# Linear attention with a gated network beside it: keys and values of two token tiles in seven block products, in rounds of two tiles

## The chip, the cores and the metric

The kernel runs on one core of one Trainium2 chip. The metric is device time in microseconds (us), the median over several runs; a second number, the span, is the time from the first to the last recorded instruction in one profiled execution.

## The reference

2048 tokens with 512 features go through a layer norm. From the normed tokens come two branches, and the output joins them. Cut to what is computed:

```python
xn = _layernorm(x)                                   # (1, 2048, 512)
qkv = xn @ wqkv                                      # H = 32 heads of Dh = 16
pq, pk = q @ w_phi, k @ w_phi                        # per head, 16 x 16
phi = concat([softmax(p), softmax(-p)], axis=-1)     # for pq and for pk
kv  = einsum("bhsf,bhsd->bhfd", phi_k, v)            # sums over all tokens
z   = einsum("bhsf->bhf", phi_k)
o   = (phi_q @ kv) / (phi_q @ z + 1e-6)
s   = o.reshape(B, S, D) @ wo
gate, up = xn @ W_gate, xn @ W_up                    # F = 1376
g   = silu((relu(gate) * up) @ W_down)
out = x + s * g
```

Everything is fp32 (the names here are shortened).

## The kernel before

**Numbers in two parts.** A TensorE (PE) matmul takes operands of type fp32r, with fewer bits than fp32. Each operand is split into a high part (a copy that rounds, on ScalarE, called ACT) and a low part (the difference, on VectorE, called DVE, or on GpSimd, called POOL). `mm3` issues three matmuls for each 128-deep piece of the contraction: low x high, high x low, high x high.

**Order.** A wrapper, `InOrder`, keeps all instructions of an engine in the order in which the program calls them. A planner, `Clock` (line 63), estimates at build time when each engine is free, with fixed costs and rates; background generators (weight preparation, queries) are advanced at `pace.pump()` where their engine is due. So the order is settled when the kernel is built, and an instruction that waits holds up whatever stands behind it on its engine. All instructions are recorded under one line (L59), so views are read by the names of tiles.

**Phase 1** runs over 16 tiles of 128 tokens (n = 0 to 15; two blocks of 512 tokens are taken alternately, `PAIRS`). Ahead of the loop (line 1091) a prologue folds `w_phi` into the key and query weights (`fold`, WK and WQ) and turns the first tiles. For each tile:

- `norm_stats`, `norm_scale`, `norm_apply`: mean and variance by two ACT passes, a power of -1/2 on POOL, and a scaled copy `xn`. Tiles 0 to 3 use `norm_vector`, with bn statistics on DVE.
- `turn` (line 320): transposes on PE into PSUM (`pxT`), high part by ACT, a full copy `xf` by ACT, low part by DVE (`lo_xt`). `sums_x` (327) makes, for each pair of tiles, four sums of the transposed blocks on POOL (`sa`, `sb`), and `sums_hi` and `sums_lo` split them. XT holds eight planes: four blocks of x (A21, A22, A11, A12) and four combinations S1 to S4. They are what the seven-product scheme of phase 2 needs.
- `project(n, WK, "pk")` and `project(n, WV, "pv")` (359): 12 matmuls of 128x512 each.
- `exponents` (391): largest and smallest of each group of 16 on DVE (`mx`), two differences (`ek`). Then ACT's exp, and in `features` (407) the value's split (`vhl`), the sum of each group (`sm`), its reciprocal written into the PSUM bank of pv, and the weighting `ek<-ek,pv`.
- `features_split` (430): high part of the features by ACT, low part by POOL (`phl`, 128x1024), and a DMA on POOL's queue that adds the features into `zacc`.
- `kv_products` (438): 16 matmuls into four PSUM banks (`pkv`), which are held from tile 0 to the end of phase 1, so that four banks rotate for everything else. The products of tile n come three tiles later from n = 10 on (`LATER = 9`), two tiles later before that.
- `query(n - 1)` (364): 12 matmuls, 24 for the first two tiles, stored by DMA.

**Phase 2** is two halves of 1024 tokens. Each runs over 11 blocks of the hidden features (f = 0 to 10): `gate_up` does gate and up together in seven block products of 6 matmuls (`pa`, `pb`, `pc`, `pd`), then `down` (`py`); the queries' features and products (`q_pair`) run beside it, and output tiles (`pso`) follow.

**Weights of phase 2.** `f_load` (457) loads the raw block f, `f_prep` (480) makes combinations (`tab`, `wa` to `wd`) and splits them, low parts on POOL, and spills the result to DRAM for half 1. `all_preps` (1073) orders that: blocks f = 2 and 3 (`AHEAD`) are prepared first, in phase 1, spilled, and loaded again when half 0 comes to them; f = 0 and 1 from tiles 12 and 15 on (`START`); the others one block ahead in half 0.

Of the kernel before, what the change touches and what calls it, by code (L numbers as in the profile page):

```python
# [7 lines left out]
F32 = mybir.dt.float32  # L8
# [5 lines left out]
P = 128  # L14
# [30 lines left out]

class InOrder:
# [113 lines left out]
def layer_kernel(ctx: ExitStack, tc: tile.TileContext, x, wkT, wqT, wv, wo, wf, cst, out):  # L160
# [24 lines left out]
    def f32(t):  # L185
        return t.bitcast(F32)
# [64 lines left out]
        return lambda: split(*map(by_parity, w[k]), even_first(p))  # L251


    mhalf = sb.tile([P, 96], F32, name="mhalf")[:, 0:1]
    XT = sb.tile([P, 8, 2, 2, BT], F32R, tag="XT", name="XT")
    pace.shared = XT.name
    XN, XF, SF = {}, {}, {}

    def norm_stats(n):
        xt = X.pop(n)  # L260
        xn = u2((P, D), "xn")
        sm, ss, rs, bias = small(1, "lm"), small(1, "lv"), small(1, "lr"), small(1, "lb")
        nc.scalar.activation(xn, xt, AF.Copy, scale=-1.0 / D, accum_out=sm)
        nc.scalar.activation(xn, xt, AF.Square, bias=sm, accum_out=ss)
        XN[n] = xn, xt, bias, rs, sm, ss

    def norm_scale(n):
        xn, xt, bias, rs, sm, ss = XN[n]
        nc.vector.tensor_scalar(rs, ss, 1.0 / D, 1e-5, op0=ALU.mult, op1=ALU.add)
        nc.gpsimd.tensor_tensor(rs, rs, mhalf, op=ALU.pow)  # L270

    def norm_apply(n):
        xn, xt, bias, rs, sm, ss = XN[n]
        nc.vector.tensor_scalar(bias, sm, rs, None, op0=ALU.mult)
        nc.scalar.activation(xn, xt, AF.Identity, bias=bias, scale=rs)
        XN[n] = xn

    def norm_vector(n):

        xt = X.pop(n)  # L280
        st, mv, rs = small(6, "bs", 2), small(2, "bm", 2), small(1, "br", 2)
        nc.vector.bn_stats(st, xt)
        nc.vector.bn_aggr(mv, st)
        nc.vector.tensor_scalar(rs, mv[:, 1:2], 1e-5, None, op0=ALU.add)
        nc.gpsimd.tensor_tensor(rs, rs, mhalf, op=ALU.pow)
        XN[n] = u2((P, D), "xn"), xt, mv, rs

    def norm_vector_apply(n):
        xn, xt, mv, rs = XN[n]
        for c in [slice(0, 256), slice(256, D)] if n == 0 else [slice(0, D)]:  # L290
            nc.vector.tensor_scalar(xn[:, c], xt[:, c], mv[:, 0:1], rs, op0=ALU.subtract, op1=ALU.mult)
        XN[n] = xn

    def cols(n):
        i = order[n][1]
# [21 lines left out]
    def lo_xt(n, p):  # L317
        add(nc.vector, xt_part(n, 1), p, f32(xt_part(n, 0)), ALU.subtract)

    def turn(m, full=True):  # L320
        p = transpose_x(m)
        hi_xt(m, p)
        if full:
            full_xt(m, p)
        return m, p

    def sums_x(n):

        x0, x1 = XF.pop(n - 1), XF.pop(n)
        sa, sb_ = u2((P, 2, 2, P), "sa"), u2((P, 2, 2, P), "sb")  # L330
        add(nc.gpsimd, sa[:, 0], x1[:, 0], x1[:, 1])
        add(nc.gpsimd, sb_[:, 0], x0[:, 0], x1[:, 0], ALU.subtract)
        add(nc.gpsimd, sa[:, 1], sa[:, 0], x0[:, 0], ALU.subtract)
        add(nc.gpsimd, sb_[:, 1], x0[:, 1], sa[:, 1], ALU.subtract)
        SF[n] = sa, sb_

    def sums_hi(n):
        for s, c in zip(SF[n], (S1, S3)):
            nc.scalar.activation(XT[:, c:c + 2, 0, :, cols(n)], s, AF.Copy)

    def sums_lo(n):
        for s, c in zip(SF.pop(n), (S1, S3)):
# [64 lines left out]
    def features(n, e, raised, pv, between):  # L407
# [14 lines left out]
        if n:  # L422
            features_scale(n, e, pv)

    def features_scale(n, e, pv):
# [29 lines left out]
    DONE = set()  # L455

    def f_load(f):
        if f == AHEAD[-1]:
# [21 lines left out]
    def f_prep(f, keep=True):  # L480
# [17 lines left out]
        yield "scalar", ta  # L498
        nc.scalar.activation(wb[0], ta, AF.Copy)
        put(f, 2, wb[0])  # L500
        yield "gpsimd", wa[0]
        for c in range(2):
            add(nc.gpsimd, wa[1][:, c], rg[c][:, :, 0, :], f32(wa[0][:, c]), ALU.subtract)
# [11 lines left out]
        yield "gpsimd", wc[0]  # L515
        add(nc.gpsimd, wc[1], tb, f32(wc[0]), ALU.subtract)
        put(f, 5, wc[1])
        fd = u2((P, D), "fdh", F32R), u2((P, D), "fdl", F32R)
        yield "scalar", rd
# [5 lines left out]
        yield "gpsimd", fd[0]  # L525
        add(nc.gpsimd, fd[1], rd, f32(fd[0]), ALU.subtract)
        put(f, 8, fd[1])
        if keep:
            FT[f], WD[f] = [wa, wb, wc, wd], fd
# [505 lines left out]
    for n in range(3, 7):  # L1035
        load_x(n)
    norm_vector_apply(0)
    px = turn(0, False)
    folds = [fold(WK, wk_raw[:, k, :], k) for k in range(2)]
    lo_xt(*px)  # L1040
    folds[0]()
# [16 lines left out]
        wv_lo(k)  # L1058
    norm_vector(2)
    full_xt(*px)  # L1060
    px = turn(1)
    lo_xt(*px)
# [5 lines left out]
    sums_x(1)  # L1068
    folds[0]()
    folds[1]()  # L1070
    norm_vector_apply(3)

    def all_preps():
        for f in AHEAD:
            f_load(f)
            yield 30,
            yield from f_prep(f, False)
        f_load(0)
# [12 lines left out]
    for n in range(N):  # L1091
        at[0] = n
        if n + 7 < N:
            load_x(n + 7)
        if n == 2:
            preps = pace.add(all_preps(), 0, 3)
        if 1 < n < N - 4:
            norm_apply(n + 4)
        if 0 < n < N - 5:
            norm_scale(n + 5)  # L1100
        if n > 1:
            pk = project(n, WK, "pk")
        if n > LATER:
            kv_products(n - 3)
            pace.pump()
        turned = [turn(n + LEAD)] if 1 < n < N - LEAD else [turn(3)] if n == 1 else []
        pace.pump()
        if turned and turned[0][0] % 2:
            sums_x(turned[0][0])
        pv = project(n, WV, "pv")  # L1110
        pace.pump()
        if n == 0:
            features(0, early, True, pv, lambda: None)
            pk = project(1, WK, "pk")
            norm_stats(4)
            norm_scale(4)
            lo_xt(*turn(2))
            features_scale(0, early, pv)
            norm_stats(5)
            sums_hi(1)  # L1120
            norm_apply(4)
            norm_scale(5)
            early = exponents(pk)
        else:
            if n == 1:
                norm_apply(5)
            features(n, early if n == 1 else exponents(pk), False, pv, lambda: [lo_xt(*t) for t in turned])
            if n == 1:
                features_split(0)
                sums_lo(1)  # L1130
            query(n - 1)
            pace.pump()
            if n == 1:
                lo_xt(*turn(4))
            if n % 2 == 0 and n - 1 < N // 2:
                pace.later(4, lambda n=n: spill_x(n - 1))
        if n + 6 < N:
            norm_stats(n + 6)
        if n % 2 and n + 2 < N:
            sums_hi(n + 2)  # L1140
        if n:
            features_split(n)
        if n % 2 and n + 2 < N:
            sums_lo(n + 2)
        if 2 <= n < LATER:
            kv_products(n - 2)
            pace.pump()


    kvacc, zB, kvhl = [None] * 3  # L1150
# [5 lines left out]
    kvt = u4((P, NG, P), "kvt")  # L1156
    nc.vector.memset(kvt, 0.0)
    q_load(0)
    for n in (N - 3, N - 2):
        kv_products(n)  # L1160
    query(N - 1)
    pace.pump()

    def state():
# [216 lines left out]
```

## Time and profile before

| | us |
|---|---|
| median of 3 runs | 563.39 |
| lowest, highest | 563.32, 564.13 |
| profiled execution | 562.88 |
| its span | 561.1 |
| tiles 2 to 15 of phase 1 (39.35 to 161.93) | 122.58 |
| half 0, from the first gate-up matmul (166.59) to half 1's first (354.95) | 188.36 |

The profile is one execution, on the one core. Busy time of an engine counts its instructions, not its waits. In rows of groups, `out<-in` names tiles, then come sizes (partitions x elements) and count; after the bar stand total busy time in us and the mean of one in ns, after the next bar the idle time ahead of them and what ended it. In rows of the timeline and the chain the first number is the start in us, the second the duration; a duration of a matmul is its latency, and one that follows another of 128x512 starts about 0.227 us later. In window rows each engine's busy time is followed by its number of instructions, then come the granted clock, the busy share of the DMA engines and GB/s. A row of DMA issues ends with the size in KB and the median time from issue to landing.

### The profile page before, as it was taken

How to read it: one execution, taken by the hardware profiler on the slowest of the kernel's cores; microseconds unless marked ns; L12 is line 12 of the kernel's file. 1: busy time of each engine (PE TensorE's matmuls, PEld its weight loads, DVE VectorE, ACT ScalarE, POOL GpSimd, SP SyncE). 2: the span in 40 equal slices, each digit the busy share in tenths (PEclk: the TensorE clock that was granted, in tenths of full speed). 3: DMA queues.
4: the chain of work that ended last, by engine and by line, in shares of the span. 5: the costliest groups of instructions: out<-in, count | busy, mean ns of one | idle time of the engine just before them, and what ended most of it. 6: DMA issues, size and time to landing. Idle time of an engine off the chain costs nothing.

```text
span 561.1 us, 8197 instructions
## 1 busy us (share of the span) xinstructions
PE 555.5 (99%) x2618; PEld 465.0 (83%) x2618; DVE 386.2 (69%) x584; ACT 303.1 (54%) x543; POOL 404.6 (72%) x347
## 2 busy tenths in 40 slices
PE   8999999999999999999999999999999999999997
PEld 8888888888888888888888888887888888888886
DVE  5978777676657897799963432799883948665323
ACT  3898687765555557456464151235465555644510
POOL 1689987899888487997978333473568786888473
PEclk9999999999999999999999999999999999999999
DMA  8358999855599817979779999991755765559874
GB/s 285 132 157 238 269 270 324 245 153 166 150 304 321 313 61 261 356 266 285 269 250 322 331 388 410 370 396 47 202 187 193 244 206 183 157 179 320 252 210 165
DMA packets 84539, 137.98 MB, mean 246 GB/s; under 512 B 7824, under 2 KB 34320, under 8 KB 83600
## 3 DMA queue, kind: packets, MB, share of 16 engines
q1 hardware_dynamic: 81040, 125.33, 64.7%
q0 software_dynamic: 3312, 12.06, 11.1%
q8 instruction: 21, 0.34, 0.2%
q14 instruction: 22, 0.18, 0.1%
q10 hardware_dynamic: 144, 0.07, 0.0%
HBM read 76.87 MB, written 52.69 MB: 231 GB/s over the span
## 4 chain that ended last, share of the span: by engine, by line
PE 93%; DVE 3%; DMA 2%; issue 0%; SPq 0%; POOL 0%
PE py L59 21%; PE pd L59 10%; PE pa L59 9%; PE pb L59 8%; PE pv L59 8%; PE pk L59 8%; PE pq L59 8%; PE pso L59 8%; PE pc L59 6%; PE pkv L59 3%; PE pnum L59 3%; PE pxT L59 1%; PE pfold L59 1%; DMA pql<-pq 1%; DMA wd<-ws 1%; DVE eq L59 1%
## 5 line engine op out<-in xcount | busy, mean ns | idle before, releaser
L59 PE MATMUL py<-fdh,hl 128*128 128x512 f32 x176 | 68.5, 389 | 0.0
L59 PE MATMUL py<-fdh,hh 128*128 128x512 f32 x176 | 68.5, 389 | 0.0
L59 PE MATMUL py<-fdl,hh 128*128 128x512 f32 x176 | 68.5, 389 | 0.0
L59 PE MATMUL pa<-XT,wa 128*128 128x512 f32 x264 | 67.0, 389 | 0.0
L59 PEld LDWEIGHTS pa<-XT,wa 128*128 128x128 f32 x264 | 49.6, 188 | 10.3
L59 DVE TENSOR_TENSOR y<-py,y 128x512 f32<-128x512 f32 x40 | 27.5, 689 | 36.5 <-PE py L59 36.5
L59 POOL TENSOR_TENSOR phl<-ek,phl 128x1024 fp32r<-128x1024 f32 x15 | 36.1, 2409 | 10.7 <-ACT phl L59 10.7
L59 PE MATMUL pv<-wvh,XT 128*128 128x512 f32 x128 | 43.5, 401 | 0.0
L59 PE MATMUL pk<-wkh,XT 128*128 128x512 f32 x128 | 42.4, 392 | 0.0
L59 POOL TENSOR_TENSOR ez<-eq,zB 128x1024 f32<-128x1024 f32 x16 | 38.5, 2415 | 4.4 <-ACT eq L59 2.0
L59 POOL TENSOR_TENSOR hl<-t,hh 128x512 fp32r<-128x512 f32 x16 | 20.8, 1298 | 27.3 <-ACT hh L59 26.3
L59 PE MATMUL pq<-XT,wqh 128*128 128x512 f32 (+1 forms) x144 | 40.3, 366 | 0.0
L59 PEld LDWEIGHTS py<-fdh,hh 128*128 128x128 f32 x176 | 33.0, 188 | 6.9
L59 PEld LDWEIGHTS py<-fdl,hh 128*128 128x128 f32 x176 | 33.0, 188 | 6.8
L59 PEld LDWEIGHTS py<-fdh,hl 128*128 128x128 f32 x176 | 33.0, 188 | 6.8
L59 POOL TENSOR_TENSOR y<-y,ys 128x512 f32<-128x512 f32 x24 | 30.9, 1291 | 9.6 <-ACT ys L59 9.6
L59 PE MATMUL pd<-XT,wd 128*128 128x512 f32 x132 | 33.8, 390 | 0.5 <-DVE t L59 0.5
L59 PE MATMUL pd<-XT,wc 128*128 128x512 f32 x132 | 33.8, 389 | 0.0
L59 POOL TENSOR_TENSOR ol<-of,oh 128x512 fp32r<-128x512 f32 (+1 forms) x13 | 20.2, 1596 | 18.9 <-ACT oh L59 18.9
L59 PE MATMUL pc<-XT,wb 128*128 128x512 f32 x132 | 33.7, 389 | 0.0
L59 PE MATMUL pb<-XT,wb 128*128 128x512 f32 x132 | 33.5, 389 | 0.0
L59 POOL TENSOR_TENSOR pTl<-ez,pTh 128x1024 fp32r<-128x1024 f32 x10 | 24.0, 2400 | 8.4 <-ACT pTh L59 8.4
(174 smaller groups left out, 1559.2 us busy)
## 6 DMA issues: line engine op xcount, KB each, us to landing
zacc<-ek POOLq DMA_DIRECT2D x15, 512.0 KB, 5.8
xts<-XT SPq DMA_DIRECT2D x4, 1792.0 KB
XT<-xts SPq DMA_DIRECT2D x7, 1024.0 KB, 20.4
wa<-ws SPq DMA_DIRECT2D x26, 256.0 KB, 3.2
wb<-ws SPq DMA_DIRECT2D x26, 256.0 KB, 4.8
wc<-ws SPq DMA_DIRECT2D x26, 256.0 KB, 5.1
ws<-wa SPq DMA_DIRECT2D x22, 256.0 KB, 4.0
ws<-wb SPq DMA_DIRECT2D x22, 256.0 KB, 4.2
```

What stands on the lines that cost most here:

```text
L59: return self.tc.keep_in_program_order(op(*a, **k))
```

## The change

Tiles 0 and 1 stay as they were but for details. From tile 2 on the loop goes by pairs, `pair(m)` for m = 1 to 7, with n = 2m and n + 1.

- In the first two pairs (m = 1, 2) keys and values of both tiles are four projections of 12 matmuls, as before. From m = `FIRST` = 3 (tile 6, the seventh) they are seven blocks of 6 matmuls: two of x's blocks with keys' weights give `py`, four combinations S1 to S4 meet weights T0 to T2 and half of WV, and A22 meets T3. ACT copies partial results to where two sums grow from one start (`px<-py`, `va`, `vb`), and DVE adds `pz` to `va` and to `vb`.
- T0 to T3, combinations of key and value weights and their parts, are made by steps listed in `PLAN` (ten on DVE, ten on POOL, eight on ACT; 128x512 each) in pairs 1 to 3.
- The order in a pair: first half of keys, two blocks (or values of n + 1), second half of keys, exponents, third block, kv(n - 2), turn of n + 3, query(n - 1), kv(n - 1), A22, exponents, S4, turn of n + 4, query(n). Features of the second tile are done at the start of the next pair.
- The norm is done in place (`xt`; ACT's first passes write into one `junk` tile), the second tile of a pair takes bn statistics on DVE from m = 3 on, and one power serves both tiles.
- `sums_x` is two DVE differences that read PSUM and two POOL sums; the full copy by ACT is made for even tiles only.
- The reciprocal of the groups' sums stays in SBUF (`rc`), exp is one instruction of 1024, and in the seven-product rounds the value's low part is made by POOL.
- `AHEAD` is empty: f = 2 and 3 are prepared in half 0 like the others. f = 0 and 1 start at tiles 14 and 15. `sums_of` gives low sums of weights to DVE or POOL: from tile 14 on whichever the planner sees free first (with 5000 units against DVE in `lighter`), in turns before that.

```diff
-AHEAD = (2, 3)
-LATER = 9
-START = (12, 15)
+AHEAD = ()
+FIRST = 3
+PLAN = {(1, "sums"): "vc50 vc51", (1, "split a"): "gc00", ...}
+START = (14, 15)
-A21, A22, A11, A12, S1, S2, S3, S4 = range(8)
+A21, A22, A11, A12, S3, S2, S1, S4 = range(8)
...
+    def turned(n, p):
+        lo_xt(n, p)
+        if n % 2:
+            sums_x(n, p)
+    def sums_x(n, p):
+        a, b = XF.pop(n - 1), u2((P, 2, 2, P), "sb")
+        add(nc.vector, b[:, 0], a[:, 0], p[:, 0], ALU.subtract)
+        add(nc.vector, b[:, 1], p[:, 1], b[:, 0], ALU.subtract)
+        SF[n] = b, a
+    def sums_more(n):
+        b, a = SF[n]
+        add(nc.gpsimd, a[:, 0], a[:, 0], b[:, 1])
+        add(nc.gpsimd, a[:, 1], a[:, 1], b[:, 1], ALU.subtract)
...
+    def features_k(n, e):
+        sm, rc = small(64, "sm", 2), small(64, "rc", 2)
+        nc.vector.tensor_reduce(sm, groups(e), op=ALU.add, axis=AX.X)
+        nc.vector.reciprocal(rc, sm)
+        nc.vector.tensor_tensor(groups(e), groups(e), rc.unsqueeze(2).to_broadcast([P, 64, DH]), op=ALU.mult)
+        EK[n] = e
...
-        yield "gpsimd", wb[0]
-        add(nc.gpsimd, wb[1], ta, f32(wb[0]), ALU.subtract)
+        yield from sums_of(wb[1], ta, f32(wb[0]), ALU.subtract, wb[0])
...
+    def sums_of(o, a, b, op=ALU.subtract, *need):
+        engine = lighter()
+        if at[0] < N - 2:
+            turns[0] += 1
+            engine = ("gpsimd", "vector")[turns[0] % 2]
+        yield engine, *(need or (a, b))
+        add(getattr(nc, engine), o, a, b, op)
+    def lighter(n=512):
+        return min(("vector", "gpsimd"), key=lambda e: max(pace.free[e], pace.now) + pace.FIXED[e] + pace.RATE[e] * n + (e == "vector") * 5000)
...
+    def pair(m):
+        n, c = 2 * m, cols(2 * m)
+        at[0] = n
+        def block(p, s, w, first):
+            mm3(p, lambda k: (XT[:, s, 0, k, c], XT[:, s, 1, k, c]), rows(w), range(2), first)
+            pace.pump()
+        if m <= NP // 2:
+            pace.later(4, lambda: spill_x(n - 1))
+        seven = m >= FIRST
+        py = ps(name="pk")
+        if seven:
+            block(py, A11, WK[:2], True)
+            px = ps(name="pk")
+            nc.scalar.activation(px, py, AF.Copy)
+        else:
+            mm3(py, xt_cols(n), rows(WK), range(KD))
+        if m > 1:
+            features_k(n - 1, EB.pop())
+        t_steps(m, "start")
+        pz = ps(name="pv")
+        if seven:
+            block(pz, S1, T[0], True)
+            block(px, S2, T[1], False)
+            va = u2((P, D), "va")
+            nc.scalar.activation(va, px, AF.Copy)
+        else:
+            mm3(pz, xt_cols(n + 1), rows(WV), range(KD))
...
+        if news:
+            norm_stats(*news, bn=m > 2)
+        if seven:
+            block(py, A12, WK[2:], False)
+        ea = exponents(py)
+        if seven:
+            block(px, S3, T[2], False)
+            vb = u2((P, D), "vb")
+            nc.scalar.activation(vb, px, AF.Copy)
+            add(nc.vector, vb, pz, vb)
+        else:
+            vb = pz
...
+        kv_products(n - 2)
+        pace.pump()
+        at[0] = n + 1
+        if n + 3 < N:
+            t = turn(n + 3)
+        exp_all(ea)
+        features_v_hi(n + 1, vb)
...
+        query(n - 1)
+        features_k(n, ea)
...
+        features_split(n)
+        t_steps(m, "split a")
+        kv_products(n - 1)
+        pace.pump()
+        if seven:
+            block(px, A22, T[3], False)
+        else:
+            px = project(n + 1, WK, "pk")
+        eb = exponents(px)
+        if seven:
+            block(pz, S4, WV[2:], False)
+            add(nc.vector, va, pz, va)
+        else:
+            va = project(n, WV, "pv")
+        if n + 4 < N:
+            t = turn(n + 4)
+            if n + 8 < N:
+                load_x(n + 8)
+        exp_all(eb)
+        t_steps(m, "turned")
+        if n + 4 < N:
+            turned(*t)
+        features_v_hi(n, va)
+        features_v_lo(n, va, nc.gpsimd if seven else nc.vector)
+        EB.append(eb)
+        query(n)
+        t_steps(m, "end")
+        pace.pump()
```

More of the change, by code (lines that the diff above doesn't have):

```diff
@@ L251, in fold @@
         return lambda: split(*map(by_parity, w[k]), even_first(p))
[L254 removed]
+    mhalf = sb.tile([P, 96], F32, name="mhalf")[:, 0:2]
     XT = sb.tile([P, 8, 2, 2, BT], F32R, tag="XT", name="XT")
@@ L500, in f_prep @@
         put(f, 2, wb[0])
-        yield "gpsimd", wa[0]
         for c in range(2):
-            add(nc.gpsimd, wa[1][:, c], rg[c][:, :, 0, :], f32(wa[0][:, c]), ALU.subtract)
+            yield from sums_of(wa[1][:, c], rg[c][:, :, 0, :], f32(wa[0][:, c]), ALU.subtract, wa[0])
         put(f, 1, wa[1])
@@ L514, in f_prep @@
         nc.scalar.activation(wd[:, 0], b22, AF.Copy)
-        yield "gpsimd", wc[0]
-        add(nc.gpsimd, wc[1], tb, f32(wc[0]), ALU.subtract)
+        yield from sums_of(wc[1], tb, f32(wc[0]), ALU.subtract, wc[0])
         put(f, 5, wc[1])
@@ L524, in f_prep @@
         put(f, 6, wd)
-        yield "gpsimd", fd[0]
-        add(nc.gpsimd, fd[1], rd, f32(fd[0]), ALU.subtract)
+        yield from sums_of(fd[1], rd, f32(fd[0]), ALU.subtract, fd[0])
         put(f, 8, fd[1])
@@ L1073, in all_preps, with t_steps @@
+    def t_steps(m, where):
+        for what in PLAN.get((m, where), "").split():
+            STEPS[0](what)
     def all_preps():
@@ L1077, in all_preps @@
             yield from f_prep(f, False)
+        while at[0] < START[0] - 1:
+            yield 3,
         f_load(0)
@@ L1090, in layer_kernel @@
     at = [0]
-    for n in range(N):
+    for n in range(2):
         at[0] = n
-        if n + 7 < N:
-            load_x(n + 7)
-        if n == 2:
+        load_x(n + 7)
+        if n == 1:
             preps = pace.add(all_preps(), 0, 3)
-        if 1 < n < N - 4:
-            norm_apply(n + 4)
-        if 0 < n < N - 5:
+            t_prep()
+        if n > 0:
             norm_scale(n + 5)
[L1101 to L1109, printed above, removed]
+        tn = turn(3) if n else None
         pv = project(n, WV, "pv")
@@ L1124, in layer_kernel @@
         else:
[L1125 to L1130, printed above, removed]
+            norm_apply(5)
+            features(n, early, False, pv, lambda: turned(*tn))
+            sums_more(3)
+            features_split(0)
+            sums_lo(1)
             query(n - 1)
             pace.pump()
-            if n == 1:
-                lo_xt(*turn(4))
@@ L1135, in layer_kernel @@
-            if n % 2 == 0 and n - 1 < N // 2:
-                pace.later(4, lambda n=n: spill_x(n - 1))
-        if n + 6 < N:
-            norm_stats(n + 6)
[L1139 to L1146, printed above, removed]
-            pace.pump()
+            turned(*turn(4))
+            sums_hi(3)
+            features_split(1)
+            sums_lo(3)
@@ L1150, in layer_kernel @@
+    EB = []
+    for m in range(1, NP):
+        pair(m)
+    features_k(N - 1, EB.pop())
+    features_split(N - 1)
     kvacc, zB, kvhl = [None] * 3
```

172 lines of the change are left out of this document (131 added, 41 removed).

## The prediction

> **What bounds the kernel now.** I read the page first (busy shares, granted clock, the chain that ended last), then the waits of TensorE (PE), whose columns are total, count and longest in us.
>
> ```profile
> PE 555.5 (99%) x2618; PEld 465.0 (83%) x2618; DVE 386.2 (69%) x584; ACT 303.1 (54%) x543; POOL 404.6 (72%) x347
> PEclk9999999999999999999999999999999999999999
> PE 93%; DVE 3%; DMA 2%; issue 0%; SPq 0%; POOL 0%
> PE pidle L59 <- DVE mhalf L59: 1.1, 1, 1.1
> PE pxT L59 <- DVE xn L59: 0.5, 1, 0.5
> PE pd L59 <- DVE t L59: 0.5, 1, 0.5
> ```
>
> PE is busy 555.5 of the 561.1 us span, at full granted clock, and holds 93% of the chain. Its waits are small: the first two of these rows lie in the prologue, the third in half 1. So a matmul that goes shortens the kernel by its issue time unless PE begins to wait, and the question for every other edit is whether a helper becomes late. How full the helpers are is read from windows: tiles 2 to 15 of phase 1, weight blocks f=3 to 8 of half 0, and the two stretches of 40 us with the densest VectorE (DVE).
>
> ```profile
> core 0: us, PE busy (x) PEld busy (x) DVE busy (x) ACT busy (x) POOL busy (x), PEclk, DMA share, GB/s
> 39.35:161.93 122.58, 122.58 (x606) 103.38 (x606) 89.88 (x135) 86.30 (x163) 111.03 (x108) 1.00 0.82 234
> 207.91:303.27 95.36, 95.36 (x430) 79.21 (x429) 73.15 (x109) 55.74 (x108) 82.07 (x81) 1.00 0.82 279
> 240.00:280.00 40.00, 40.00 (x178) 33.06 (x177) 37.10 (x56) 21.46 (x41) 35.44 (x34) 1.00 0.82 274
> 360.00:400.00 40.00, 39.54 (x173) 31.89 (x172) 36.50 (x53) 18.90 (x30) 22.06 (x12) 1.00 0.70 242
> ```
>
> In phase 1 GpSimd (POOL) is the fullest helper, 111.03 of 122.58 or 91%; DVE has 73%. In f=3 to 8 DVE has 77% (73.15 of 95.36) and POOL 86%. PE never waits in either. The last two rows are my scale for a full in-order helper: DVE at 93% (37.10 of 40) cost PE nothing, at 91% (36.50 of 40) it cost 0.46 us.
>
> **Removed: matmuls.** Rounds m=3 to 7 (tiles 6 to 15) replace four projections of 12 matmuls by seven blocks of 6: 42 for 48, five times.
>
> ```profile
> 58.59 2.75 PE pk L59 x12
> 68.21 2.75 PE pk L59 x12
> 166.59 1.36 PE pa L59 x6
> ```
>
> A block of 6 takes 1.36 us, so five rounds save 5 x 1.36 = **6.8 us**. A tile takes 68.21 - 58.59 = 9.62 us now, a pair 19.2, a seven-round 17.9. No other edit changes the number of matmuls.
>
> **Moved: the kv products of the first tiles.** Pair 1 runs key of tile 2, value of tile 3, kv(0), the transposes of tile 5, query(1), kv(1). The kv(1) that stood at 47.84 now follows query(1) directly.
>
> ```profile
> 29.55 2.75 PE pk L59 x12
> 32.74 2.77 PE pv L59 x12
> 35.51 2.87 PE pq L59 x24
> 39.35 2.75 PE pk L59 x12
> 47.84 1.11 PE L59 MATMUL pkv<-phl,vhl 128*128 128x256 f32 x8
> 33.34 2.41 POOL L59 TENSOR_TENSOR phl<-zacc,phl 128x1024 fp32r<-128x1024 f32 x1 [0.21 <-ACT phl L59]
> 38.25 2.41 POOL L59 TENSOR_TENSOR phl<-ek,phl 128x1024 fp32r<-128x1024 f32 x1
> ```
>
> From 29.55: key 2.75, value 2.77, kv(0) 0.96 and transposes 0.44 (the two lie in 32.30 to 32.74 and 38.38 to 39.35 now), query 2.87, so kv(1) is wanted at 39.3. It needs the low part of phl(1) from POOL, which ends at 38.25 + 2.41 = 40.66; POOL's order up to it stays phl(0), two low sums, phl(1). That is 1.3 us of wait, and kv(0), wanted at 35.1, already waits 0.7 of it for phl(0) (33.34 + 2.41 = 35.75). To this comes a later start: the two new differences of tile 1 on DVE (0.42 us each, the 128x256 row below) stand ahead of the statistics and scaling of tile 3, and PE already waits 0.5 us for xn. I take 0.3 for it: **1.6 us** lost (1.1 to 2.0). Behind the waiting matmul on PE's queue stands key of tile 3, so the wait is on the path; nothing in a full PE gives it back.
>
> **Moved onto DVE: the pair rounds.** What DVE does for a tile, by its rows:
>
> ```profile
> L59 DVE TENSOR_REDUCE mx<-pk 128x32 f32<-128x512 f32 x32 | 20.5, 683 | 7.5 <-PE pk L59 7.5
> 14.32 0.68 DVE L59 TENSOR_TENSOR ek<-pk,mx 128x512 f32<-128x512 f32 x1
> 14.92 0.68 DVE L59 TENSOR_TENSOR ek<-mx,pk 128x512 f32<-128x512 f32 x1
> L59 DVE TENSOR_REDUCE sm<-ek 128x64 f32<-128x1024 f32 x16 | 19.3, 1208 | 0.0
> L59 DVE TENSOR_TENSOR ek<-ek,pv 128x1024 f32<-128x1024 f32 x15 | 18.3, 1220 | 0.5
> L59 DVE RECIPROCAL pv<-sm 128x64 f32<-128x64 f32 x16 | 9.0, 561 | 0.6
> L59 DVE TENSOR_TENSOR XT<-pxT,XT 128x512 fp32r<-128x512 f32 x16 | 11.0, 689 | 6.7 <-ACT xf L59 5.5 <-ACT XT L59 1.2
> 18.98 0.69 DVE L59 BATCH_NORM_STATS2 bs<-xt 128x6 f32<-128x512 f32 x1
> L59 DVE TENSOR_TENSOR kvacc<-pkv,kvacc 128x256 f32<-128x256 f32 x4 | 1.4, 417 | 0.6 <-ACT kvacc L59 0.6
> ```
>
> Exponents and features of a tile are 2 x 0.683 + 2 x 0.68 + 1.208 + 0.561 + 1.220 = 5.7 us, of a pair 11.4. A seven-round adds two low parts of x (1.4), two differences (0.8), the sums va and vb (1.4) and one statistic (0.7): 15.7. Neighbours start 0.60 apart at 0.68 each (14.32, 14.92), which takes off 0.08 at some 20 places, and six tiny ones add 0.8: about 14.9 of 17.9 us, 83%. POOL has two phl (2 x 2.41), four low sums of x and v at (38.25 - 33.34 - 2.41) / 2 = 1.25, two sums at 0.74 (below), two transfers into zacc and a power (0.7):
>
> ```profile
> L59 POOL DMA_DIRECT2D zacc<-ek x15 | 13.2, 883 | 1.2 <-DMA zacc<-ek 1.2
> ```
>
> That is 13.8 us or 77%, less than now, since weight preparation leaves these rounds. Two rounds are fuller: m=2, with seven of the ten DVE steps for the combined weights (7 x 0.60), has 18.4 of 19.2 (96%); m=7, with six weight sums (four of 512, two of 256 elements) and a third weighting, 19.2 of 20.6 (93%). The tightest new wait is query(n-1), which takes the PSUM bank of py and so waits for exponents on DVE: these need 0.4 + 2.5 us after py, and block S3, kv products and transposes in between give 1.36 + 0.95 + 0.44 = 2.75. So a seven-round alone costs nearly nothing, and what it costs is set by how long DVE trails. One DMA bears on that. SP now loads x(n+8) only after the last transposes of the pair, and in rounds 3 and 4 the bn statistics of that tile stand on DVE ahead of the exponents of py.
>
> ```profile
> xt<-x SPq DMA_DIRECT2D x16, 256.0 KB, 5.5
> xt<-x SPq DMA_DIRECT2D x4, 256.0 KB, 7.9
> ```
>
> The first row is the whole span, the second the stretch from 60 to 160 us, with the spills of x on the same queue. From the transposes the query (2.7) and four blocks (5.4), less the statistic's own 0.7, are cover, 7.4 us: nothing is lost at 5.5, 0.5 twice at 7.9. By the 93% row the fuller rounds cost nothing; I take **1.0 us** for all seven rounds (0 to 8.7, the upper end from the contention below).
>
> **Moved onto DVE: weight preparation in half 0.** Of the low sums of f=0 to 10 DVE takes 17 of 512 and 9 of 256 elements, about 17 x 0.60 + 9 x 0.34 = 13.3 us. For f=2 and 3 the spills and reloads in phase 1 go, and their preparation comes in half 0. Laid out in program order, f=3 to 8 hold 8.3 us of these sums, and 6.2 us of query work that comes one block later. DVE goes from 73.5 to about 88.7 of 93.4 us, 95%, single blocks 98%. By the 93% row this is free. By the 91% row it is 0.46 per 40 us, 1.1 in all. If the 2.9 us per 40 that DVE idled even in the densest stretch (7%, 6.5 us here) stay, DVE ends at 95.2, 1.8 us late. I take **1.0 us** (0 to 2.1, the end again that of the contention). POOL is relieved of these, so it isn't next. The dropped transfers free the DMA queues (share 0.82), on which PE does not wait; I count them at nothing, since no row shows a wait to be gained.
>
> **Sum.** The profiled execution took 562.88 us, 0.51 below the median of the runs shown. 562.88 - 6.8 + 1.6 + 1.0 + 1.0 = 559.7, on the median's scale **560.2 us**.
>
> **A price that no row settles: DVE beside POOL.** The new DVE work reads two SBUF tensors: the weighting by a reciprocal now in SBUF (before: in PSUM), the weight steps, the weight sums. Before, wide operations of this kind ran only at the end, without POOL. The nearest rows are one scaling, alone and beside POOL:
>
> ```profile
> 19.99 0.54 DVE L59 TENSOR_SCALAR xn<-xt,bm,br 128x512 f32<-128x512 f32 x1
> 21.64 0.99 DVE L59 TENSOR_SCALAR xn<-xt,bm,br 128x512 f32<-128x512 f32 x1
> 21.60 0.74 POOL L59 TENSOR_TENSOR sb<-xf 128x256 f32<-128x256 f32 x1
> 552.82 0.69 DVE L59 TENSOR_TENSOR y<-y,sx 128x512 f32<-128x512 f32 x1
> ```
>
> The scaling takes 0.54 while POOL is idle or at one element, and 0.99 beside a wide sum on POOL, x1.83; a sum of two SBUF tensors without POOL takes 0.69, as long as one that reads PSUM. The lower bound is thus x1.0, the upper x1.83. I take the value near the lower one, since 0.69 is the row of the same operation and the row of x1.83 is of another, faster one: what is not fast may have less to lose.
>
> The Trainium skill ("GPSIMD Engine Reference", section "Key points") says that GpSimd shares its SBUF interfaces with VectorE, and names as contended the DVE instructions in a two-port mode or with two SBUF inputs. That speaks against this change, and by it the time would be that of the first rival; the pair 0.54 and 0.99 agrees with it for the scaling, and no row of before shows a two-input sum beside POOL.
>
> **Rivals.** *Slower, by contention.* If every two-input DVE operation costs x1.83, m=2 adds 0.83 x (7 x 0.60 + 2 x 1.17) = 5.4 and has 23.8 us of DVE for 19.2 of PE, 4.6 late; m=7 adds 5.5, 24.7 for 20.6, 4.1 late; f=3 to 8 adds 6.8, 95.5 for 93.4, 2.1 late. Together 10.8, and with the prologue 12.4 against 6.8 saved: 563.4 + 5.6 = 569.0. It decides as soon as 6.3 of the 10.8 is paid (6.8 - 1.6 + 1.1). For it: the 0.99 row. Against it: 0.69 for two-input sums, no faster than others. Chance 0.19. *No change.* PE pays the prologue at its upper end (2.0), 1.8 in half 0 and about 2 in the rounds: 563.4 - 6.8 + 5.8 = 562.4. Chance 0.13. *All of it.* phl(1) comes earlier, because the wait before phl(0) shrinks or POOL's two fewer sums move it up, and nothing else waits: 563.4 - 6.8 = 556.6. Against it stands the idle of only 0.21 ahead of phl(0), which ACT sets. Chance 0.12, within faster. *The forecast*, 556.9 to 562.2: 0.56.
>
> **How the numbers follow.** About 0.2% (1.1 us) is what a measurement can tell from no change. Faster: 0.56 + 0.12 = 0.68; same 0.13; slower 0.19. The range begins at the floor less half the spread of the shown runs, 556.2, and reaches into the contention case as far as half of its 10.8 beside the prologue, 563.4 - 6.8 + 1.6 + 5.4 = 563.6, and 1 us beyond for the upper end of the prologue and of half 0, 564.6; the remainder of that case, some 0.15, lies above.
>
> **What would show it.** Right: PE's busy time 548.7 us (555.5 - 6.8); a wait of pkv on POOL's phl of 1 to 2 us near 40 us; seven-rounds of 17.9 us; few waits of PE on DVE in f=3 to 8. Wrong: the weighting of 128x1024 at 2 us instead of 1.2, or weight sums at 1.2 instead of 0.69; a wait list of PE headed by DVE's ek, vb or t7; rounds m=2 or m=7 much longer than 19.2 and 20.6.

## The result, and the profile after

The changed kernel takes 587.69 us (585.34 to 589.90, 4 runs) against 563.36 us for the kernel before beside it (563.32 to 564.13): 24.3 us or 4.3% slower, ratio 1.0428, 95% interval 1.0386 to 1.0469. The forecast was 560.2, in a range that ended at 564.6. The profiled execution took 589.9 us, with a span of 588.1.

The page of the changed kernel, in the rows that answer to those of before:

```profile
PE 562.0 (96%) x2588; PEld 464.6 (79%) x2588; DVE 456.6 (78%) x646; ACT 307.8 (52%) x536; POOL 398.7 (68%) x315
PEclk9999969899997999999999999999999999999999
PE 50%; DVE 11%; POOL 3%; issue 3%; DMA 3%; ACT 2%; SPq 0%; POOLq 0%; DVEq 0%; ACTq 0%
```

Its longest waits of PE (total, count, longest):

```profile
PE pk L60 <- DVE ek L60: 6.5, 3, 3.7
PE pkv L60 <- POOL vhl L60: 4.1, 1, 4.1
PE pv L60 <- DVE XT L60: 2.7, 1, 2.7
PE pkv L60 <- POOL phl L60: 1.8, 3, 1.1
PE pd L60 <- DVE t L60: 1.8, 3, 0.8
PE pv L60 <- DVE sb L60: 1.7, 1, 1.7
```

PE has 30 matmuls less and yet is busy 6.5 us longer, at a clock that is no longer full everywhere; it waits, mostly for DVE; and it holds 50% of the last chain, not 93%. DVE is busy 70.4 us longer (456.6 against 386.2), POOL 5.9 us less. Where the time went is seen from windows between the same points of the work: first key projection, fifth key projection (first of pair 2 after the change), first gate-up matmul, first of half 1. The first three rows after the header are the kernel before, the other five the changed one, which is cut once more at the start of pair 4 and of pair 7.

```profile
core 0: us, PE busy (x) PEld busy (x) DVE busy (x) ACT busy (x) POOL busy (x), PEclk, DMA share, GB/s
10.04:48.80 38.76, 38.76 (x232) 34.01 (x230) 33.46 (x61) 33.56 (x68) 29.81 (x31) 1.00 0.60 196
48.80:166.42 117.62, 117.62 (x586) 99.44 (x585) 84.92 (x126) 80.60 (x150) 105.06 (x101) 1.00 0.81 231
166.42:354.78 188.36, 188.36 (x843) 156.37 (x842) 125.09 (x186) 91.82 (x172) 134.72 (x123) 1.00 0.85 297
10.81:53.28 42.47, 39.73 (x231) 33.78 (x230) 41.12 (x69) 31.84 (x62) 27.97 (x27) 1.00 0.54 176
53.28:104.99 51.71, 41.74 (x186) 33.41 (x187) 47.14 (x59) 30.48 (x54) 37.23 (x30) 0.90 0.62 169
104.99:160.24 55.25, 55.25 (x267) 46.32 (x267) 49.15 (x69) 37.28 (x60) 43.91 (x33) 0.97 0.45 107
160.24:187.68 27.44, 21.97 (x104) 18.16 (x103) 26.72 (x26) 14.29 (x26) 23.83 (x21) 0.93 0.83 248
187.68:381.68 194.00, 191.62 (x844) 156.91 (x843) 149.73 (x214) 96.72 (x184) 126.15 (x109) 0.99 0.82 284
```

The spans differ by 27.0 us: 0.8 before the first key projection, 3.7 in the prologue and pair 1 (42.47 for 38.76), 16.8 from there to half 0 (51.71 + 55.25 + 27.44 = 134.40 for 117.62, although 6.8 us of matmuls are gone), 5.6 in half 0, and 0.1 in half 1. Within phase 1, pairs 4 to 6 have no wait of PE, though pair 4 begins at a lowered clock; the loss is in pairs 2 and 3 and in pair 7.

What DVE does in that time is in its groups, with POOL's phl for comparison:

```profile
L60 DVE TENSOR_TENSOR ek<-ek,rc 128x1024 f32<-128x1024 f32 x14 | 38.8, 2774 | 0.5
L60 DVE TENSOR_TENSOR t<-wvr 128x512 f32<-128x512 f32 x2 | 6.2, 3118 | 0.0
L60 DVE TENSOR_TENSOR l<-wvr,h 128x512 fp32r<-128x512 f32 x3 | 3.7, 1271 | 0.0
L60 DVE TENSOR_TENSOR wb<-tab,wb 128x512 fp32r<-128x512 f32 x11 | 12.3, 1122 | 2.8 <-ACT wb L60 2.8
L60 DVE TENSOR_TENSOR fdl<-rawd,fdh 128x512 fp32r<-128x512 f32 x8 | 8.9, 1110 | 0.6 <-ACT fdh L60 0.6
L60 DVE TENSOR_TENSOR XT<-pxT,XT 128x512 fp32r<-128x512 f32 x16 | 11.0, 687 | 4.6 <-ACT XT L60 2.7 <-ACT xf L60 1.9
L60 POOL TENSOR_TENSOR phl<-ek,phl 128x1024 fp32r<-128x1024 f32 x15 | 36.8, 2455 | 27.4 <-ACT phl L60 22.0 <-DVE ek L60 5.3
```

The weighting, 1.22 us before, takes 2.77; steps on combined weights and weight sums of 512 elements take 1.1 to 3.1 on average in these rows, where a sum of this size in a quiet place took 0.69. What reads one tensor from PSUM is as before (XT<-pxT,XT: 0.687). The timeline shows what such an instruction waits for. DVE in pair 3:

```profile
95.38 1.21 DVE L60 TENSOR_REDUCE sm<-ek 128x64 f32<-128x1024 f32 x1
97.21 5.00 DVE L60 TENSOR_TENSOR ek<-ek,rc 128x1024 f32<-128x1024 f32 x1
```

POOL beside it:

```profile
96.72 1.93 POOL L60 TENSOR_TENSOR XT<-sb,XT 128x512 fp32r<-128x512 f32 x1
98.16 1.73 POOL L60 TENSOR_TENSOR XT<-xf,XT 128x512 fp32r<-128x512 f32 x1
99.41 1.71 POOL L60 TENSOR_TENSOR vhl<-vb,vhl 128x512 fp32r<-128x512 f32 x1
```

POOL works without a pause until 99.41 + 1.71 = 101.12. The weighting ends at 97.21 + 5.00 = 102.21, 1.09 us after that: nearly its whole work of 1.22 lies behind POOL's run. The sum of one tensor (sm<-ek), at the same time as POOL, takes its usual 1.21.

Not every weighting waits so long. In pair 4 one meets two POOL instructions and gets in between them:

```profile
118.66 1.30 POOL L60 TENSOR_TENSOR XT<-sb,XT 128x512 fp32r<-128x512 f32 x1
118.93 2.10 DVE L60 TENSOR_TENSOR ek<-ek,rc 128x1024 f32<-128x1024 f32 x1
119.91 2.27 POOL L60 TENSOR_TENSOR XT<-xf,XT 128x512 fp32r<-128x512 f32 x1
```

It ends 1.07 us after the first POOL instruction (119.96), and the second one, which began 0.05 us before that end, takes 2.27 us instead of 1.30: here POOL waits for DVE. Of the 14 weightings nine end 1.1 us after a single POOL instruction, one meets none, and four wait through four or five (4.34 to 5.72 us each, half of the 38.8 us). In those four each further POOL instruction had begun at least 0.25 us before the end of the one ahead of it, as above at 98.16 and 99.41. Nearly all such meetings in the other runs divide in the same way; what makes POOL's instructions overlap was not tried.

### The profile page after: what moved, and what is told of

Its sections match the earlier page's. It is cut to its first block, busy times and chain, and to the rows that moved or that the text cites. A ratio compares the mean times of both kernels' runs of the same rounds, so it can differ in the third digit from the quotient of the medians.

```text
span 588.1 us, 8118 instructions
## 1 busy us (share of the span) xinstructions
PE 562.0 (96%) x2588; PEld 464.6 (79%) x2588; DVE 456.6 (78%) x646; ACT 307.8 (52%) x536; POOL 398.7 (68%) x315
## 4 chain that ended last, share of the span: by engine, by line
PE 50%; DVE 11%; POOL 3%; issue 3%; DMA 3%; ACT 2%; SPq 0%; POOLq 0%; DVEq 0%; ACTq 0%
PE py L60 15%; PE pd L60 8%; PE pso L60 7%; PE pa L60 7%; PE pb L60 6%; PE pc L60 4%; PE pnum L60 2%; DVE eq L60 2%; DVE qs L60 1%; POOL ez L60 1%; DVE ek L60 1%; DMA ws<-wb 1%; DVE qd L60 1%; DVE wb L60 1%; DMA ws<-wc 1%
## 5 line engine op out<-in xcount | busy, mean ns | idle before, releaser
L60 PE MATMUL pa<-XT,wa 128*128 128x512 f32 x264 | 68.4, 394 | 0.0
L60 DVE TENSOR_TENSOR ek<-ek,rc 128x1024 f32<-128x1024 f32 x14 | 38.8, 2774 | 0.5
L60 PE MATMUL pk<-wkh,XT 128*128 128x512 f32 x88 | 31.6, 411 | 6.5 <-DVE ek L60 6.5
L60 DVE TENSOR_TENSOR y<-pso,y 128x512 f32<-128x512 f32 x14 | 9.7, 692 | 28.4 <-PE pso L60 28.4
```

Source lines behind the costliest of these rows:

```text
L60: return self.tc.keep_in_program_order(op(*a, **k))
```

## The experiments

Theory A: a DVE instruction that reads two SBUF tensors makes no progress while POOL works. Theory B: the order of the pairs, with its few PSUM banks, makes the waits. Theory C: DVE and POOL share at a fixed rate. Times are medians; each stands against the kernel before on the same chip, 563.1 to 563.5 us in these runs.

**Reciprocal into PSUM.**

```diff
-sm, rc = small(64, "sm", 2), small(64, "rc", 2)
+sm, rc = small(64, "sm", 2), ps((P, BT), name="rc")[:, 0:64]
```

> The changed kernel with one edit: the reciprocal of the groups' sums goes into a PSUM bank, so that the 14 weightings ek<-ek,rc read one SBUF tensor instead of two. Theory A (a DVE instruction with two SBUF inputs makes no progress while POOL works): the weighting falls from 2.77 to 1.2-1.3 us, the 21.7 us of DVE that this frees take away most waits of PE in pairs 1 to 3 and part of those in pair 7, the granted clock rises, and the time falls from 587.7 to 566-574; what stays is due to weight steps and weight sums, which still read two SBUF tensors. Theory B (the order of the pairs, with its few PSUM banks, makes the waits, and long weightings are beside the point): the time stays within 1% of 587.7, or rises, since a bank more is in turn. Theory C (DVE and POOL share, each at a fixed fraction): as A for the weighting, and the weight sums stay near a constant factor, never above twice their 0.69.

586.28 us, 1.4 less than the changed kernel, with overlapping runs (584.73 to 586.72 against 585.34 to 589.90): a miss for A's time, which lies where B put it, and a hit for A's mechanism. The group of weightings in this run:

```profile
L60 DVE TENSOR_TENSOR ek<-ek,rc 128x1024 f32<-128x1024 f32 x14 | 17.1, 1221 | 0.5
```

DVE's timeline, then POOL's, where one of the longest instructions stands:

```profile
70.05 1.22 DVE L60 TENSOR_TENSOR ek<-ek,rc 128x1024 f32<-128x1024 f32 x1
71.44 6.16 DVE L60 TENSOR_TENSOR l<-wvr,h 128x512 fp32r<-128x512 f32 x1
```

```profile
74.43 2.60 POOL L60 TENSOR_TENSOR phl<-ek,phl 128x1024 fp32r<-128x1024 f32 x1
```

And PE's waits:

```profile
PE pk L60 <- DVE sb L60: 4.4, 1, 4.4
PE pk L60 <- DVE th L60: 4.1, 1, 4.1
PE pk L60 <- DVE ek L60: 3.0, 1, 3.0
```

The weighting is back at 1.22 us, in the middle of a POOL run. The next two-input instruction, a weight step, then meets the same run: 6.16 us for a work of 0.69, ending at 77.60, 0.57 after POOL's phl (77.03). DVE was freed of one long wait and went into the next; another step, th, took 6.77 us. PE waits for such a step or for what stands behind it (sb, th, ek). The lengthening belongs to the operand's place, but one such instruction on an in-order engine is enough to make PE late. C, with its fixed factor, falls here: the lengths of the steps go from 1.0 to nearly 10 times 0.69.

**All weight sums on POOL.** (`sums_of` always gives "gpsimd".)

> The changed kernel with all low sums of weights on POOL (none on DVE). Theory A: the waits of PE in pair 7 and in weight blocks f=4 to 8 (8.8 us in all, and some 4 us of lowered clock behind them) go in part, the weightings of 128x1024 stay long or grow, since POOL is fuller: 578-585 us. Theory B: no change in pairs 1 to 3, and a gain of at most 3 us. If POOL becomes the bound instead, PE waits on POOL's wb, wa or fdl in half 0 and the time is 590 or more.

593.61 us, 6 slower than the changed kernel, above A's range and where the expectation put POOL as the bound. Pairs 1 to 3 wait as before, the weightings rise to 3.07 us, and half 0 gets a new wait, not for POOL's wb, wa or fdl, as expected there, but for the queries' pTh on ACT; that a fuller POOL makes these late is argued, not shown. A group and a wait of this run:

```profile
L60 DVE TENSOR_TENSOR ek<-ek,rc 128x1024 f32<-128x1024 f32 x14 | 43.0, 3069 | 0.5
```

```profile
PE pnum L60 <- ACT pTh L60: 4.6, 4, 1.5
```

So the longer POOL works, the longer the weighting waits, as A says; and half 0 became longer (201.76 us from its first gate-up matmul to half 1's, 194.00 in the changed kernel) with DVE relieved and POOL fuller.

**No seven block products.** (`FIRST = 9`, `PLAN = {}`.)

> The changed kernel without seven block products and without the steps that make combined weights: pairs of tiles with four projections of 12 matmuls throughout. PE has 6.8 us more to do. Theory A: the steps' waits in pairs 2 and 3 go (about 10 us of waits and lowered clock), the long weightings stay, and so do pair 7 and half 0: 580-587. Theory B (the seven-product rounds themselves with their order cause the loss): below 575. If the steps cost nothing: 594.

574.33 us: 13.4 less than the changed kernel, with 6.8 us of matmuls more. The seven-product part thus cost 13.4 net, 20.2 gross. The number lies in B's range, not in A's, so this run alone would speak for the order of the rounds. But the weightings fall here as well, to 2.04 us on average, with no steps on POOL; what the rounds cost without steps is told by the borrowed weights below.

**The kernel before, with the reciprocal in SBUF.** One edit to the kernel before.

```diff
-        nc.vector.reciprocal(pv[:, 0:64], sm)
+        rc = small(64, "rc", 2)
+        nc.vector.reciprocal(rc, sm)
+        RC[n] = rc
...
-        nc.vector.tensor_tensor(groups(phi), groups(e), pv[:, 0:64].unsqueeze(2).to_broadcast([P, 64, DH]), op=ALU.mult)
+        nc.vector.tensor_tensor(groups(phi), groups(e), RC.pop(n).unsqueeze(2).to_broadcast([P, 64, DH]), op=ALU.mult)
```

> The kernel before with one edit: the reciprocal goes into SBUF instead of PSUM, so that the 15 weightings read two SBUF tensors. Nothing else differs. Theory A: each weighting waits for the run of POOL instructions that it meets; POOL is busy 91% of phase 1, so the mean rises from 1.22 to 2.5-4 us with single ones above 4, DVE is over 90% busy in phase 1 and PE begins to wait: 567-580 us against 563.4. Theory C (fixed fraction): 2.0-2.3 us for every one, DVE at 82%, PE does not wait: 563-565. Theory B: 1.22 us and 563.4.

574.51 us, ratio 1.0199 (1.0183 to 1.0214): where a reciprocal lies costs 11.4 us. Group, wait and the window of phase 1 from tile 3 on in this run:

```profile
L59 DVE TENSOR_TENSOR ek<-ek,rc 128x1024 f32<-128x1024 f32 x15 | 50.4, 3361 | 0.5
```

```profile
PE pk L59 <- DVE ek L59: 5.5, 6, 1.6
```

```profile
40.82:176.27 135.45, 128.85 (x632) 107.66 (x633) 118.92 (x136) 84.16 (x162) 118.88 (x107) 1.00 0.76 216
```

1.22 became 3.36 us, in single cases between 1.23 and 5.96, and DVE is busy 88% of that window (118.92 of 135.45). All of A's figures came but one (DVE was to be over 90% busy); the times of B and C (563 to 565) are far off. This run settles A against B and C for the weighting: PE, DVE, ACT and POOL run the same instructions in the same order as before, and only the place of the reciprocal differs.

**Pairs only.** The pair loop with no DVE instruction on two SBUF tensors in the pairs: reciprocal in PSUM, four projections in each pair, weight preparation as before the change.

> The changed kernel's pair loop with nothing on DVE that reads two SBUF tensors beside POOL: reciprocal in a PSUM bank, four projections of 12 matmuls in every pair, no combined weights, and weight preparation as in the kernel before (f=2 and 3 ahead, f=0 and 1 from tiles 12 and 15, low sums on POOL). As many matmuls as before. Theory A: the waits of the run with the reciprocal in PSUM (13.6 us in pairs 1 to 3) and of half 0 are gone, what is left is the wait of kv products on POOL's phl near 36 to 41 us and what is late behind it, 1 to 3 us: 564-566.5 us. Theory B (the order of the pairs and their PSUM banks): 570 or more.

570.65 us, 4 above A's range and just in B's. DVE's waits are gone; half 0 has none. Left are 2.9 us up to the fifth key projection (51.73 against 48.80), and one wait in pair 2, with lowered clock behind it (1.7 us):

```profile
64.08 1.22 PE L60 MATMUL pkv<-phl,vhl 128*128 128x256 f32 x8 [2.60 <-POOL phl L60]
```

**Pairs only, cleaned.** In pair 2 POOL already had weight sums of f=2 ahead of phl.

```diff
     def all_preps():
+        while at[0] < 6:
+            yield 3,
...
-    turned(*turn(1))
+    px1 = turn(1)
+    lo_xt(*px1)
...
-    sums_more(1)
...
     norm_vector_apply(3)
+    sums_x(*px1)
+    sums_more(1)
```

> The pairs-only run with two edits. The preparation of f=2 begins only at tile 6 (before: in the first pair), so that POOL has no weight sums while pairs 1 and 2 run; and in the prologue the two DVE differences of tile 1 come after the statistics and scalings of tiles 2 and 3. If the rest of 7.3 us in the pairs-only run is POOL's weight sums ahead of phl in pair 2 (2.6 us of wait and 1.7 us of lowered clock behind it) and DVE's lateness in the prologue (2.3 us), the time is 563.5-566. If it is the order of kv products and PSUM banks in the pairs, the waits move and the time stays at 569 or more.

566.71 us, 3.9 less: the wait in pair 2 was the weight sums. It is 0.7 above the range, since the edit in the prologue gained nothing: from the third key projection to the fifth PE still takes 22.00 us instead of 19.50. These 2.5 us and one wait of 1.0 us in pair 5, for POOL's phl, are the rest; that much is left to B, the order of the pairs.

**Borrowed weights.** (The pairs-only run with `FIRST = 3`, no steps, and `T.update({0: WK[:2], 1: WV[:2], 2: WK[2:], 3: WV[2:]})`.)

> As the pairs-only run, with seven block products from the seventh tile on, and with other weights of the same size in the place of the combined ones, which are not made: the steps for T0 to T3 are left out of the computation. 30 matmuls less. Theory A: the rounds themselves cost nothing more, so the time is that of the pairs-only run less 6.8 us: 557.5-560. Theory B (banks, copies and sums of the seven-product rounds make PE wait): less than half of the 6.8 is gained, 561.5 or more.

568.57 us, 2.1 less than pairs only: a miss for A, and in B's range. Weight preparation of f=2, 3, 0 and 1 stands on a POOL with shorter rounds, and PE waits for ACT's pk and va and for POOL's vhl. So I moved the preparation out of the rounds:

**Borrowed weights, preparation late.** (No block ahead, `START = (14, 15)`, prologue as in the cleaned run.)

> Seven block products from the seventh tile on with borrowed weights (the steps for T0 to T3 are left out of the computation), reciprocal in a PSUM bank, no weight preparation before tile 14, low sums on POOL. If rounds of seven products cost nothing but their matmuls once POOL and DVE have room, the stretch from the fifth key projection to tile 14's takes 6.8 x 4/5 = 5.4 us less than in the cleaned pairs-only run (96.8 us there, with one wait of 1.2), so 89-91.5 us, with no wait of PE in it. If copies, banks or sums of the rounds make PE wait, over 93. The whole time is no measure, since half 0 is then short of POOL.

The stretch, first in this run, then in the cleaned pairs-only run:

```profile
51.49:142.25 90.76, 90.76 (x454) 76.45 (x452) 73.84 (x119) 62.74 (x103) 63.50 (x52) 1.00 0.64 166
51.80:148.63 96.83, 95.84 (x477) 80.82 (x476) 74.33 (x119) 63.99 (x109) 81.87 (x76) 1.00 0.88 253
```

90.76 us with PE busy all the time, 6.1 less, of which 1.0 is the other run's wait: four rounds give 5.1 us of the 5.4 expected. Copies, banks and sums of the rounds cost almost nothing once DVE and POOL have room. These two runs leave out the making of T0 to T3. The whole run takes 572.78, since half 0 is short of POOL, as expected.

**Only the weight preparation changed, in the kernel before.** First with sums shared out as in the change, then with all on POOL.

> The kernel before with only the change's weight preparation: no blocks ahead, f=0 and 1 from tiles 14 and 15, low sums of weights on DVE or POOL as the change gives them out. Theory A (two-input DVE work beside POOL): weight sums take 1.0-1.2 us instead of 0.69, DVE trails in f=4 to 8, and PE loses there what the changed kernel loses, 3 to 5 us in half 0: 566-569. My forecast's price for this step was 1.0 us, which would give 564.4.

> As the run before it, with all low sums on POOL: what is changed is only when the preparation comes. If POOL has room for two more blocks in half 0, 563-564.5. By the run of the changed kernel with all sums on POOL, which waited 6 us in f=9, it has not: the queries that POOL serves come late and PE waits in f=6 and f=9: 568-573.

576.57 us (ratio 1.0234, 1.0219 to 1.0249), 7.6 above the range, and 579.38 us (1.0284, 1.0248 to 1.0321), 6.4 above. A group and waits of the first, then a wait of the second:

```profile
L59 DVE TENSOR_TENSOR wb<-tab,wb 128x512 fp32r<-128x512 f32 x9 | 12.2, 1361 | 1.0 <-ACT wb L59 1.0
```

```profile
PE pb L59 <- POOL wb L59: 4.6, 1, 4.6
PE pd L59 <- DVE t L59: 1.7, 3, 0.8
```

```profile
PE pnum L59 <- ACT pTh L59: 3.7, 4, 1.5
```

Put into the kernel before by itself, this part costs 13.2 and 16.0 us, nearly all of it in half 0 (201.14 and 203.06 us against 188.36). With shared sums, weights of f=1 come 4.6 us late and DVE trails in f=4 to 8; with all on POOL, weights of f=1 come late by 1.7 and 1.5 us and queries in f=9. The move of two blocks out of phase 1 costs whichever engine takes them, which the forecast did not see. The second run has no weight sum on DVE, so the price of two SBUF operands can't be its reason. Why half 0 loses more than twice the 5.6 us of the changed kernel stays open.

**The change without two-input work beside POOL.** Reciprocal in PSUM, four seven-product rounds, all twenty weight steps on POOL in pairs 1 to 4, and DVE's weight sums with a PSUM operand:

```diff
+        if engine == "vector":
+            yield "scalar", *(need or (a, b))
+            h = ps(o.shape, name="ph")
+            nc.scalar.activation(h, b, AF.Copy)
+            yield "vector", h
+            add(nc.vector, o, a, h, op)
+            return
```

> A version of the whole change without DVE instructions on two SBUF tensors beside POOL: reciprocal in a PSUM bank; seven block products from the ninth tile on (four rounds, 5.4 us of matmuls less); all twenty steps of the combined weights on POOL, spread over pairs 1 to 4; f=0 and 1 from tiles 13 and 14; a low sum of weights that goes to DVE reads its high part from a PSUM bank, into which ACT copies it. Theory A: DVE's weight sums take 0.7 us instead of 1.1, the waits in pairs 1 to 3 fall under 5 us, and the time is 558-566, where POOL, which is planned at over 100% in pair 7 and near 90% in pairs 2 and 3, sets what is lost. Theory B (order and banks): 570 or more, since two kinds of bank more are in turn.

> The run with all combined-weight steps on POOL and four seven-product rounds, tuned by its own waits: the two steps on ACT ahead of va are later in the fourth pair, the differences of tile 1 later in the prologue, weight sums from tile 14 on may go to DVE with a PSUM operand, and DVE is given more of them. By the waits of that run 1.6 us in pair 4, about 3 us in pair 7, 3 us in f=9 and 1 to 2 us in the prologue can go: 562-568 us. Below 562 it would beat the kernel before; at 570 or more POOL's load as a whole, not single places, is the limit.

572.60 and 571.11 us, both above the ranges that A gave; 570 or more was expected under B in the first and under POOL's load as a whole in the second. A group of the first:

```profile
L60 DVE TENSOR_TENSOR fdl<-rawd,ph 128x512 fp32r<-128x512 f32 x6 | 4.1, 677 | 0.1
```

The sums with a PSUM operand take 0.68 us, so A's mechanism holds for them. That POOL's load then sets the end is argued; where I took a wait away in the second run another came (for va 2.2, for wa ahead of a query 2.0, for th 1.4 us). No version that I ran beats the kernel before; the nearest, at 566.71, has neither the seven-product rounds nor the new preparation.

## Why the prediction was wrong

**The step that failed: the price of DVE beside POOL.** The mechanism was named as the first rival, with a chance of 0.19, but its size was taken from one scaling at x1.83, and the forecast took almost none of it, because 0.69 was "the row of the same operation". That row had no POOL beside it, so it said nothing on the question. Measured: x2.27 on average for the weighting (2.77 for 1.22), and up to 6.77 us for a step of 0.69. A factor was the wrong form: the price is the rest of the POOL instruction that is met, and the rest of the run where POOL's instructions overlap; POOL is busy 72 to 87% of pairs 2 to 7. Even the rival's 569.0 lay 18.7 us below the measured time.

The kernel before did have such rows, contrary to the prediction's "no row of before shows a two-input sum beside POOL". A small sum of the queries, `qd<-qs`, reads two SBUF operands:

```profile
401.47 0.22 DVE L59 SCALAR_TENSOR_TENSOR qd<-qs 128x64 f32<-128x64 f32 x1
377.03 1.29 POOL L59 TENSOR_TENSOR hl<-u,hh 128x512 fp32r<-128x512 f32 x1
377.65 0.74 DVE L59 SCALAR_TENSOR_TENSOR qd<-qs 128x64 f32<-128x64 f32 x1
```

It takes 0.22 us while POOL is idle. The other seven stand beside POOL and take 0.49 to 0.77, and each ends 0.1 us after a POOL instruction does. So the wait could be seen before the change.

The Trainium skill has this ("SBUF — State Buffer", section "SBUF: two separate sides"): the port pair that VectorE and GpSimd share is held for a whole instruction by the one that starts first, also between a DVE instruction with two SBUF inputs and a GpSimd instruction that reads SBUF, and the other is blocked. The pair of 2.10 and 2.27 us agrees; the rows of 5.00 and 6.16 us go further, since there DVE was blocked through four POOL instructions. I had weighed only that there is contention, not that it is a lock.

**Pair rounds: 1.0 us forecast.** From pair 2 to half 0 the changed kernel loses 16.8 + 6.8 = 23.6 us against its own matmuls. The load sums were close for undisturbed durations; DVE was then filled by waits as well as work (busy 47.14 of 51.71 us in pairs 2 and 3, some 12.6 of it beyond those durations).

**Half 0: 1.0 us forecast.** 5.6 us in the changed kernel. I judged it by a stretch where DVE at 93% cost PE nothing, with DVE instructions that keep their duration; weight sums did not (1.1 for 0.69). But that is not shown to be the cause: in the two versions where the sums took 0.68, half 0 still lasted 195.53 and 191.67 us against 188.36, though these differ in more than the sums. That POOL could not have taken them either, the forecast did not ask; so this term's failure is shown, its split between the engines is not.

**Prologue: 1.6 us forecast.** 3.7 in the changed kernel, with two weight steps on DVE in it that take 6.2 us; 2.5 in the cleaned pairs-only run. kv products wait for phl, as named, but only 0.4 and 0.3 us, at 36.3 and 41.1; the larger wait, for DVE's late differences of x behind them (1.7 in the changed kernel, 0.7 in the cleaned run), was not named.

**Matmuls: 6.8 us less.** Right in kind. Pairs 5 and 6 of the changed kernel take 35.56 us together, 17.8 each as forecast (17.9), with PE busy throughout, and the late-prepared borrowed weights give 5.1 us in four rounds.

**The lowered clock was not in the forecast.** After its longer waits PE is granted less:

```profile
75.00:80.00 5.00, 2.14 (x6) 1.58 (x6) 5.00 (x6) 5.00 (x9) 2.82 (x2) 0.82 1.02 310
80.00:90.00 10.00, 7.30 (x21) 5.46 (x20) 7.81 (x10) 3.09 (x5) 5.80 (x5) 0.58 0.42 105
105.00:110.00 5.00, 5.00 (x15) 3.99 (x16) 4.23 (x5) 3.30 (x6) 4.53 (x3) 0.66 0.35 86
180.00:190.00 10.00, 5.94 (x22) 4.84 (x21) 9.15 (x15) 6.00 (x11) 6.24 (x4) 0.70 0.90 257
```

These rows hold or follow waits of 3.7, 2.7, 2.4 and 4.1 us. PE busy times one minus the clock gives 0.4 + 3.1 + 1.7 + 1.8 = 7.0 us. PE is busy 562.0 instead of the 548.7 that its matmuls need; the other 6.3 us are not traced. The cleaned pairs and the last version, with waits of at most 1.0 and 2.2 us, have a clock of 1.00. The longest wait alone does not decide, though. The kernel before with late preparation on POOL falls to 0.50 for 5 us amid waits of 1.5, 1.2 and 0.7 us (317 to 324 us), and the first borrowed run stays at 1.00 after a wait of 2.6 us. That waits cause the dips was not tried by itself. The Trainium skill ("TensorE: Matmul & The Clock Gate", Part 1) has TensorE fall to half its clock after an idle window of about 3.4 us; the stretches after 3.7 and 4.1 us agree (0.50 at 80 to 85 and at 185 to 190 us, inside the rows above), while here 2.4 us, or three shorter waits in a row, went before a dip too.

## What to carry to other kernels

Before work is moved to DVE, look where each operand lies: in this kernel an instruction with two SBUF tensors beside a busy POOL cost at least the rest of the POOL instruction that it met, and the rest of the run where POOL's instructions overlapped, on top of its duration in a quiet place; one PSUM operand took that price away. A small instruction of the same kind in the old profile can show the price before the move. A row that was measured without the rival for the resource is no bound for the case with it. And when work leaves a stretch, ask of both candidate engines where it lands; a PE that never waits can hide two helpers that are nearly full.

## What was not expected of the hardware

Whether DVE gets in between two POOL instructions goes with how they follow one another: where the next one began 0.05 us before the end of the first, a weighting got in and POOL's next took 2.27 us instead of 1.30; where it began 0.25 us or more before, DVE waited on, and a step took 6.16 us. A POOL phl that met a DVE step took 2.82 us instead of 2.41. And 11.4 us, 2% of this kernel, hang on whether each tile's 128x64 reciprocal is written to PSUM or to SBUF.
